# Two FFN2 pieces of the second block put ahead of those that need the last piece of w_out, and another planned length for the tails' loads

## The chip, the core and the metric

The kernel runs on one core of one Trainium2 chip. A core has a matrix engine (TensorE, PE in the profile; its weight loads are a row of their own, PEld), VectorE (DVE), ScalarE (ACT), GpSimd (POOL), and SyncE (SP), which here only issues DMAs. Matmuls write to PSUM, of which this kernel uses two banks for attention scores and six buffers, called f, for everything else. The metric is the time of one execution on the device in microseconds.

## The reference

Eight sequences of 576 positions with eight heads of 64 go through a retention layer (attention without a softmax, with a decay by distance), and its 4608 rows of 512 through a two-layer network with an ELU between.

```python
scores = scale * np.matmul(q, k.transpose(0, 1, 3, 2))
gamma = 1.0 - 2.0 ** (-5.0 - np.arange(H, dtype=np.float32))
Dmat = np.where(rel >= 0, gamma[:, None, None] ** rel[None, :, :], 0.0)
attn_out = np.matmul(scores * Dmat[None, :, :, :], v)
x = np.ascontiguousarray(attn_out.transpose(0, 2, 1, 3)).reshape(B * S, H * D)
h = x @ w_in                                                  # 512 -> 2048
g = np.where(h > 0.0, h, alpha * (np.exp(np.minimum(h, 0.0)) - 1.0))
return (g @ w_out).astype(np.float32)                         # 2048 -> 512
```

## The kernel before

**Items.** The attention is cut into items: an item is 256 positions of four heads of one sequence. Item n is loaded (q, k, v by three DMAs, or six halves from item 8 on), q and k are scaled by powers of the decay into bf16 (`qkn`, mostly on GpSimd, line 507), v is cast (`vn`, line 561), and q and k are turned into `qkT`: on TensorE for items 0 to 6 (lines 574 and 580), by a transposing DMA from SyncE for the rest (line 618). An item's step on TensorE (S5, S6, ... in the code, function `stretch`) computes scores (`sc`), the state that is carried from one part of the sequence to the next, and the output of the item before; from item 8 on two items share a step. VectorE multiplies the scores with the mask into `pt` (line 953, or 947 from item 8 on). The last 64 positions of each sequence, the tails, are two further items, 32 and 33, whose tiles lie in a buffer called `aside`. The attention output is cast into `xt`, the input of the network.

**Blocks.** The network works on blocks of 256 rows (the first six) or 512 rows, and a block T of the tails ahead of the last one. `ffn1` makes one piece of the hidden layer into an f buffer (eight matmuls of 256 columns, or four of 512), ScalarE takes the exponential (`e`, line 1161), ScalarE or VectorE a max with zero in place (lines 1169 and 1171), and VectorE combines both into `g` in bf16 (line 1176), after which the f buffer is free. `ffn2` multiplies 128 rows of g with w_out: 16 matmuls of 512 columns into one f buffer, issued as pieces of 4 (or of 2, for block 0), and ScalarE copies the sum out (line 1216) for a store by SyncE. The first eight outputs are held back in `aside` tiles and stored much later.

**Weights.** w_in and w_out come in four pieces each by DMAs that GpSimd issues and that cast to bf16 on the way. Piece n of w_out holds the rows that the matmuls 4n to 4n + 3 of each output need. FFN2 of block 0 goes through all eight of its pieces c = 0 to 7 for both of its 128-row halves in turn, so c = 6 and 7 need the last piece of w_out.

**Order.** The program does not run in the order in which it is written. Every step is an `Op` with a cost on each engine that may do it, what it depends on, and a rank. `Plan.run` plays the steps through an event list with these costs: whenever an engine is free, it takes the ready step of the lowest rank for which a buffer of each class is free (`SLOTS`, line 245; six for f), and the steps are emitted in the order in which this play began them. That fixes the order on each engine, which engine does a step that several could do, and which buffer it gets; the hardware then keeps each engine's order and waits where the data is late. All `ffn2` pieces are tied into one sequence (line 1209: each may begin only once the piece written before it has begun), and so are the loads on SyncE. A DMA has a planned length, the first number of its `dma=`: the time for which it holds its share of the DMA engines in the play. For a tail load it stands in line 467.

The two places that are edited are line 467 and the loops over `ffn2` at lines 1312 to 1324. `seq` begins with blocks 0 and 1, `TOGETHER` is 1, `rank` is the block's rank.

Of the kernel before, what the change touches and what calls it, by code (L numbers as in the profile page):

```python
# [37 lines left out]
class Plan:  # L38
# [6 lines left out]
    def add(self, *a, **kw):  # L45
        op = Op(*a, **kw)
        self.ops.append(op)
        for key in op.use:
            self.users.setdefault(key, []).append(op)
            op.turn += self.owner.get(key, [])  # L50
        for cls, key, *_ in op.take:
            self.owner[key] = [op]
            if cls not in FREE and key not in LONE:
                op.turn += self.takers.get(cls, [])
                self.takers[cls] = [op]
        return op
# [156 lines left out]
AFTER = {"ldq0_10": "tr7"}  # L213
RANKS = {"be2": 60, "be3": 60}
TOGETHER = 1
EARLY = 5
LOOSE = True
TAILS = 1
# [35 lines left out]
def kernel(  # L254
# [32 lines left out]
    def mm(*a, **kw):  # L287
        return pin(nc.tensor.matmul(*a, **kw))  # L288
# [77 lines left out]
    def T(cls, key, shape, dt):  # L366
        return (cls, key, shape, dt)

    holds, chain = [], {}
# [5 lines left out]
    for b in ORDER:  # L375
        for r in range(FT if isinstance(b, int) else 1):
            it = Item()
# [10 lines left out]
    seq = [*range(2 * NARROW), *range(2 * NARROW, 2 * B, 2)]  # L388
# [67 lines left out]
    def load_tail(it):  # L456
        n = it.n
        it.ld = {}

        def load(name, cls, key, rows, src, b, first):  # L460
            def emit(op):
                pin(nc.sync.dma_start(tiles[key][rows * ST : (rows + 1) * ST],
                                      src[b, :, FT * P :, :].rearrange("h p d -> p h d")))

            chain[0] = add(name, {"SP": 0.63}, [], emit, len(plan.ops),
                           take=[T(cls, key, [P, H, D], FP32)] if first else [], use=[] if first else [key],
                           dma=(0.93, 32), after=chain.get(0))
            return chain[0]

        for m in range(2):  # L470
            for j in range(2):
                for i, src in enumerate((q, k)):
                    it.ld[i, m, j] = load(f"ldt{i}{m}{j}{n}", "rqt", ("rqt", n, m, j), i, src, 4 * it.t + 2 * m + j, i == 0)
            for j in range(2):
                it.ld["v", m, j] = load(f"ldt2{m}{j}{n}", "rvt", ("rvt", n, m), j, v, 4 * it.t + 2 * m + j, j == 0)
# [3 lines left out]
    def load_w_in(n0, n1, after):  # L479
        c = slice(n0 * 512, n1 * 512)  # L480

        def emit(op):
            pin(nc.gpsimd.dma_start(w_in_sb[:, :, c], moe_w_in[:, c].rearrange("(j p) n -> p j n", p=P)))  # L483

        op = add(f"wi{n0}", {"POOL": 0.8}, [], emit, -1000, dma=(2.62 * (n1 - n0), 32 * (n1 - n0), PIECE), after=after)
        for n in range(n0, n1):
            w_in_ld[n] = op
# [619 lines left out]
    def early(it):  # L1107
        n = it.n
        it.sc = ("sc", n)
        sc = add(f"sc{n}", {"PE": 0.3}, it.turned, lambda op: do_scores(it), it.rank,  # L1110
                 take=[T("sc", ("sc", n), [P, 2, 512], FP32)], use=[("qkT", n)])
        mask_step(it, sc)
        keys = [("st", n, c) for c in range(2)]
        views = [(keys[c], 0, lambda c=c: tiles[keys[c]][:, :P]) for c in range(2)]
        st = add(f"st{n}", {"PE": 0.25}, [it.cq[1, 0], it.cq[1, 1], it.cv], lambda op: do_state(it, views), it.rank + 1,
                 use=[("qkn", n), ("vn", n)])
        reserve(st, keys)
        after_state(it, st, views, [(keys[0], 0), (keys[1], 0)])
# [62 lines left out]
    def rows_of(blk, it):  # L1181
        if blk == "T":
            return [(j * ST, ST, (2 * it + j) * S + FT * P) for j in range(2)]
        row = blk // 2 * S + blk % 2 * TB + it * P
        if (blk, it) in HALVED:
            return [(0, ST, row), (ST, ST, row + ST)]
        return [(0, P, row)]
# [3 lines left out]
    def ffn2(blk, it, c, per, rank, n0=0, n1=DM):  # L1191
        pkey, okey = ("p", blk, it, n0), ("ot", blk, it, n0)
        wide, cols = width[blk] > TB, n1 - n0
        gs = range(c * per, (c + 1) * per) if wide else range(c * per // 2, (c + 1) * per // 2)

        def emit(op):
            pm = tiles[pkey][:, :cols]
            for ft in range(c * per, (c + 1) * per):
                if wide:
                    g = tiles["g", blk, ft]  # L1200
                else:
                    g = tiles["g", blk, ft // 2][:, ft % 2 * TB : (ft % 2 + 1) * TB]
                mm(pm, g[:, it * P : (it + 1) * P], w_out_sb[:, ft, n0:n1], start=(ft == 0), stop=(ft == NFT - 1))

        op = add(f"F2_{blk}_{it}_{c}_{n0}", {"PE": 0.216 * per * cols / DM},
                 [gdone[blk, pp] for pp in gs] + [w_out_ld[c * per // 4]], emit, rank,
                 take=[T("f", pkey, [P, DM], FP32)] if c == 0 else [],
                 use=([pkey] if c else []) + [("g", blk, pp) for pp in gs], after=chain.get(2))
        chain[2] = op
        if (c + 1) * per == NFT:  # L1210
            late = len(deferred) < DEFER and blk != "T"
            if late:
                deferred.append(okey)

            def emit_o(op):
                pin(copy[op.eng](tiles[okey][:, :cols], tiles[pkey][:, :cols]))  # L1216

            oc = add(f"oc_{blk}_{it}_{n0}", {"ACT": 0.59 if cols == DM else 0.15 + cols / 1200,
                                             "DVE": (0.66 if cols == DM else 0.1 + cols / 960, 0.3)}, [op], emit_o, rank,
                     take=[T("late" if late else "ot", okey, [P, DM], FP32)], use=[pkey], banks=[(pkey, 0)])  # L1220

            for lo, n, i0 in rows_of(blk, it):
                def emit_s(op, lo=lo, n=n, i0=i0):
                    pin(nc.sync.dma_start(out[i0 : i0 + n, n0:n1], tiles[okey][lo : lo + n, :cols]))

                so = add(f"so_{blk}_{it}_{n0}_{lo}", {"SP": 0.46}, [oc], emit_s, -2, use=[okey],
                         dma=(0.67 * n / P * cols / DM, 8))
                if late:
                    so.at = DEFER_AT + 2.0 * len(deferred)
# [57 lines left out]
    add("warm", {"PE": 3.0}, [], emit_warm, -10 ** 6, take=[T("f", "warm", [P, 512], FP32)])  # L1287
    for it in items[:EARLY]:
        early(it)
        early_out(it)  # L1290
    for n in range(4):
        load_w_in(n, n + 1, None)
    prev, left = [], items[EARLY:]
    while prev or left:
# [13 lines left out]
    for i, blk in enumerate(seq):  # L1308
        if i > 1:
            for p in range(NFT if width[blk] > TB else NP):  # L1310
                ffn1(blk, p, base[blk] + 2 * p)
        rank = base[blk] + width[blk] // 16 + 1
        if i < TOGETHER:
            if i == 0:
                for c in range(8):
                    for b in seq[:TOGETHER]:
                        for it in range(2):
                            ffn2(b, it, c, 2, rank + 2 * c)
        else:
            for it in range(width[blk] // P):  # L1320
                cuts = LAST if (i, it) == (len(seq) - 1, width[blk] // P - 1) else (0, DM)
                for n0, n1 in zip(cuts, cuts[1:]):
                    for c in range(4):
                        ffn2(blk, it, c, 4, rank + 8 * it + 2 * c, n0, n1)

    for op in plan.ops:
# [74 lines left out]
```

## Time and profile before

| | us |
|---|---|
| median of 3 runs | 299.19 (299.08 to 302.05) |
| the profiled execution | 299.32 |
| its span, first to last instruction | 297.6 |
| TensorE busy | 291.2 |
| ScalarE busy | 197.9 |
| VectorE busy | 181.1 |
| GpSimd busy | 133.7 |
| moved by DMA | 50.12 MB |

The granted TensorE clock is 1.0 throughout. A row of a timeline gives the start, the time from the first start to the last end, engine, line, operation, what is written and read, shapes, and how many instructions of the kind followed one another; in brackets stands the idle time of the engine before it and what ended it. The end of a matmul is modelled and overlaps the start of the next, so distances are better taken from start to start. A row of the table of waits gives who waited for whom, the sum in us, how often, and the longest. A row of the table by windows gives the stretch and its length, then busy time and count of PE, PEld, DVE, ACT and POOL, the granted clock, the DMA share and GB/s. "To landing" is the time from the issue of a DMA to the arrival of its data.

### The profile page before, as it was taken

How to read it: one execution, taken by the hardware profiler on the slowest of the kernel's cores; microseconds unless marked ns; L12 is line 12 of the kernel's file. 1: busy time of each engine (PE TensorE's matmuls, PEld its weight loads, DVE VectorE, ACT ScalarE, POOL GpSimd, SP SyncE). 2: the span in 40 equal slices, each digit the busy share in tenths (PEclk: the TensorE clock that was granted, in tenths of full speed). 3: DMA queues.
4: the chain of work that ended last, by engine and by line, in shares of the span. 5: the costliest groups of instructions: out<-in, count | busy, mean ns of one | idle time of the engine just before them, and what ended most of it. 6: DMA issues, size and time to landing. Idle time of an engine off the chain costs nothing.

```text
span 297.6 us, 8805 instructions
## 1 busy us (share of the span) xinstructions
PE 291.2 (98%) x3518; PEld 162.3 (55%) x3518; DVE 181.1 (61%) x323; ACT 197.9 (66%) x393; POOL 133.7 (45%) x253
## 2 busy tenths in 40 slices
PE   7999989999999999999999999999999999999996
PEld 3578646765776664545545454545454544444445
DVE  5999924947856948697855946466550169643300
ACT  2679624858767758778786868686772289777512
POOL 5961279956755856567442827372533000000000
PEclk9999999999999999999999999999999999999999
DMA  7999999989999999999999998976577310011132
GB/s 205 273 205 214 216 274 226 194 181 170 182 178 195 196 231 209 184 223 213 247 255 260 214 191 203 210 176 150 125 161 176 73 35 4 0 35 36 37 106 71
DMA packets 142010, 50.12 MB, mean 168 GB/s; under 512 B 120721, under 2 KB 137489, under 8 KB 141969
## 3 DMA queue, kind: packets, MB, share of 16 engines
q1 hardware_dynamic: 137744, 45.37, 71.3%
q0 software_dynamic: 4224, 4.19, 8.4%
q8 instruction: 27, 0.44, 0.6%
q14 instruction: 15, 0.11, 0.1%
HBM read 36.70 MB, written 9.44 MB: 155 GB/s over the span
## 4 chain that ended last, share of the span: by engine, by line
PE 85%; DMA 7%; DVE 3%; POOL 2%; issue 1%; ACT 0%; ACTq 0%; DVEq 0%
PE f L288 83%; DMA w_out_sb<-in_moe_w_out_dram 7%; PE sc L288 2%; DVE pt L953 1%; POOL w_out_sb L491 1%; PE f L574 1%; POOL w_in_sb L483 1%; DVE g L1176 0%; DVE qkn L507 0%; DVE qkT L580 0%; DVE s_mid L850 0%; POOL s_mid L836 0%; POOL s_end L836 0%; DVE f L1171 0%; ACT e L1161 0%
## 5 line engine op out<-in xcount | busy, mean ns | idle before, releaser
L288 PE MATMUL f<-w_out_sb,g 128*128 128x512 bf16 (+2 forms) x608 | 141.2, 368 | 1.0 <-DMA w_out_sb<-in_moe_w_out_dram 1.0
L288 PE MATMUL f<-xt,w_in_sb 128*128 128x256 bf16 (+1 forms) x768 | 138.4, 326 | 0.4 <-DVE g L1176 0.4
L1176 DVE SCALAR_TENSOR_TENSOR g<-e,f 128x512 bf16<-128x512 f32 x144 | 95.4, 683 | 65.2 <-ACT f L1169 51.5
L1161 ACT ACTIVATE e<-f 128x512 f32<-128x512 f32 x144 | 84.6, 597 | 35.2 <-PE f L288 27.0
L288 PEld LDWEIGHTS <-w_in_sb 128*128 128x128 bf16 x768 | 74.5, 98 | 54.2 <-DVE g L1176 0.9
L288 PEld LDWEIGHTS <-g 128*128 128x128 bf16 x608 | 56.6, 98 | 58.8 <-issue 1.3
L1169 ACT ACTIVATE f<-f 128x512 f32<-128x512 f32 x113 | 66.6, 592 | 0.0
L507 POOL TENSOR_TENSOR qkn<-rqk,far_k 128x256 bf16<-128x256 f32 x48 | 29.0, 611 | 11.4 <-DMA rqk<-in_k_dram 10.6
L507 POOL TENSOR_TENSOR qkn<-rqk,far_q 128x256 bf16<-128x256 f32 x48 | 28.7, 611 | 6.0 <-DMA rqk<-in_q_dram 5.1
L1216 ACT COPY ot<-f 128x512 f32<-128x512 f32 (+2 forms) x30 | 16.9, 562 | 20.5 <-PE f L288 20.4
L561 POOL CAST vn<-rv 128x512 bf16<-128x512 f32 x28 | 17.0, 609 | 20.2 <-DMA rv<-in_v_dram 20.0
L893 POOL CAST y<-mid 64x256 bf16<-64x256 f32 x33 | 12.8, 398 | 25.4 <-DVE mid L878 8.9
L988 ACT CAST xt<-f 128x512 bf16<-128x512 f32 x24 | 12.9, 589 | 15.1 <-PE f L288 15.1
L1171 DVE TENSOR_SCALAR f<-f 128x512 f32<-128x512 f32 x31 | 21.3, 694 | 2.5 <-ACT e L1161 2.4
L947 DVE TENSOR_TENSOR pt<-sc,mask_t 128x1024 bf16<-128x1024 f32 x12 | 14.6, 1219 | 3.2 <-PE sc L288 3.2
L893 ACT CAST y<-mid 64x256 bf16<-64x256 f32 x33 | 12.8, 402 | 1.8 <-DVE mid L878 0.9
L634 POOL TENSOR_TENSOR aside<-aside,gq 128x256 bf16<-128x256 f32 x16 | 9.4, 611 | 10.0 <-DMA aside<-in_k_dram 9.8
L507 POOL TENSOR_TENSOR qkn<-rqk,gq 128x256 bf16<-128x256 f32 x12 | 7.4, 630 | 11.9 <-DMA rqk<-in_q_dram 11.9
L878 DVE TENSOR_TENSOR mid<-f,mid 128x256 f32<-128x256 f32 x24 | 10.2, 424 | 2.5
L288 PE MATMUL f<-pt,vn 64*64 64x64 bf16 (+1 forms) x512 | 11.6, 202 | 0.0
L953 DVE TENSOR_TENSOR pt<-sc,mask 128x1024 bf16<-128x1024 f32 x8 | 9.8, 1222 | 2.0 <-PE sc L288 1.9
L288 PE MATMUL f<-zero 128*128 128x512 bf16 (+3 forms) x30 | 9.2, 416 | 1.3 <-DVE zero L293 1.3
(91 smaller groups left out, 165.6 us busy)
## 6 DMA issues: line engine op xcount, KB each, us to landing
rqk<-in_q_dram SPq DMA_DIRECT2D x48, 128.0 KB, 3.2
rqk<-in_k_dram SPq DMA_DIRECT2D x48, 128.0 KB, 3.5
rv<-in_v_dram SPq DMA_DIRECT2D x48, 128.0 KB, 3.5
out_dram<-ot SPq DMA_DIRECT2D x18, 256.0 KB, 3.1
out_dram<-ot SPq DMA_DIRECT2D x19, 128.0 KB, 2.3
rqk<-in_q_dram SPq DMA_DIRECT2D x8, 256.0 KB, 6.0
rqk<-in_k_dram SPq DMA_DIRECT2D x8, 256.0 KB, 5.5
rv<-in_v_dram SPq DMA_DIRECT2D x8, 256.0 KB, 5.4
```

Source lines behind the costliest of these rows:

```text
L288: return pin(nc.tensor.matmul(*a, **kw))
L507: pin(alu[op.eng].tensor_tensor(dst, tiles[raw][:, :, e], g, ALU.mult))
L561: pin(copy[op.eng](tiles["vn", n], tiles["rv", n]))
L893: pin(copy[op.eng](dst, tiles[key][j * D : (j + 1) * D]))
L947: pin(nc.vector.tensor_tensor(tiles[it.pt].rearrange("p i h n -> p (i h n)")[:, : 2 * w * C].rearrange("p (i x n) -> p i x n", i=2, n=C), ...
L953: pin(nc.vector.tensor_tensor(tiles["pt", n].rearrange("p i h n -> p (i h) n"), tiles[it.sc].rearrange("p i (h n) -> p (i h) n", h=2), mas ...
L988: pin(copy[op.eng](by_block(it.xt)[:, 2 * it.T + c], tiles[xkey, c].rearrange("p (h n) -> p h n", n=P)))
L1161: pin(nc.scalar.activation(tiles[ekey], tiles[hkey], AF.Exp))
L1169: pin(nc.scalar.activation(ph, ph, AF.Relu))
L1171: pin(nc.vector.tensor_scalar_max(ph, ph, 0.0))
L1176: pin(nc.vector.scalar_tensor_tensor(tiles[gkey], tiles[ekey], -1.0, tiles[hkey], ALU.add, ALU.min))
L1216: pin(copy[op.eng](tiles[okey][:, :cols], tiles[pkey][:, :cols]))
```

## The change

Two pieces of the first 128 rows of block 1, four matmuls each with the first two pieces of w_out, are written ahead of pieces c = 6 and 7 of block 0, with a rank that lies just ahead of theirs, and left out of their old place. Apart from that, the planned length of a tail load goes from 0.93 to 0.8; it is a number of the play alone, and the DMA moves the same bytes.

```diff
@@ -213,6 +213,7 @@
 TOGETHER = 1
+HEAD = 2
 EARLY = 5
@@ -464,7 +465,7 @@
             chain[0] = add(name, {"SP": 0.63}, [], emit, len(plan.ops),
                            take=[T(cls, key, [P, H, D], FP32)] if first else [], use=[] if first else [key],
-                           dma=(0.93, 32), after=chain.get(0))
+                           dma=(0.8, 32), after=chain.get(0))
             return chain[0]
@@ -1313,6 +1314,8 @@
         if i < TOGETHER:
             if i == 0:
                 for c in range(8):
+                    for k in range(HEAD if c == 6 else 0):
+                        ffn2(seq[1], 0, k, 4, rank + 11)
                     for b in seq[:TOGETHER]:
                         for it in range(2):
                             ffn2(b, it, c, 2, rank + 2 * c)
@@ -1320,7 +1323,7 @@
             for it in range(width[blk] // P):
                 cuts = LAST if (i, it) == (len(seq) - 1, width[blk] // P - 1) else (0, DM)
                 for n0, n1 in zip(cuts, cuts[1:]):
-                    for c in range(4):
+                    for c in range(HEAD if (i, it) == (1, 0) else 0, 4):
                         ffn2(blk, it, c, 4, rank + 8 * it + 2 * c, n0, n1)
```

Since the play is one, the order changes beyond the two pieces. TensorE has the same instructions in both kernels; up to the moved pieces its order is the same, and behind them FFN1 pieces, FFN2 pieces and items' steps change places at some forty points to the end. Of the steps that more than one engine may do, one max pass goes from VectorE to ScalarE and two casts of attention states go from GpSimd to ScalarE. On SyncE, loads, transposes and stores swap places at some twenty points from item 9 on.

## The prediction

> **What bounds the kernel now.** I read the page's busy shares and its chain first, then who TensorE waited for, then TensorE's own timeline around each wait.
>
> ```profile
> span 297.6 us, 8805 instructions
> PE 291.2 (98%) x3518; PEld 162.3 (55%) x3518; DVE 181.1 (61%) x323; ACT 197.9 (66%) x393; POOL 133.7 (45%) x253
> ...
> PE 85%; DMA 7%; DVE 3%; POOL 2%; issue 1%; ACT 0%; ACTq 0%; DVEq 0%
> ```
>
> ```profile
> PE f L288 <- DMA w_out_sb<-in_moe_w_out_dram: 1.0, 1, 1.0
> PE f L288 <- DVE g L1176: 0.4, 1, 0.4
> ```
>
> ```profile
> 222.41 12.25 PE L288 MATMUL f<-w_out_sb,g 128*128 128x512 bf16 x56
> 234.49 0.40 PE L288 MATMUL f<-aside,s_end 128*128 128x64 bf16 x8
> ```
>
> TensorE is busy for 98% of the span, and the chain that ended last runs through it for 85%. After the start-up its table of waits holds two entries that cost anything: one for the last piece of w_out, one for VectorE's g. The last two rows, from TensorE's timeline, say what saturated means: 56 matmuls of 512 columns in 234.49 - 222.41 = 12.08 us, so one starts every 0.216 us; a piece of FFN2 (four matmuls) is 0.863 us. Work moved about on TensorE costs nothing and gains nothing; only a filled wait counts, and only if no new one opens. With the start-up alike, the gain is bounded by the two waits.
>
> The Trainium skill ("Perfetto Trace Analysis", Identifying the Most-Contended Engine) says that matmul busy time is a poor measure and that the share of LDWEIGHTS should be taken; by its 55% TensorE would have much room, and a filled wait could be swallowed elsewhere. The 0.216 us pitch speaks against that here, so I carry a filled wait through to the end.
>
> **The first wait.**
>
> ```profile
> 38.97 0.61 PE L288 MATMUL f<-w_out_sb,g 128*128 128x512 bf16 x2
> 40.55 1.89 PE L288 MATMUL f<-w_out_sb,g 128*128 128x512 bf16 x8 [0.97 <-DMA w_out_sb<-in_moe_w_out_dram]
> 42.27 0.39 PE L574 MATMUL f<-ident,qkn 128*128 128x128 bf16 x4
> 42.49 1.03 PE L288 MATMUL f<-w_out_sb,g 128*128 128x512 bf16 x4
> ...
> 44.53 0.42 PE L288 MATMUL sc<-qkT 64*64 64x128 bf16 x16
> ...
> 45.01 0.40 PE L574 MATMUL f<-ident,qkn 128*128 128x128 bf16 x4
> ...
> 47.20 0.27 PE L288 MATMUL f<-qkT,s_mid 128*128 128x128 bf16 x2
> ```
>
> ```profile
> 18.81 21.69 DMA w_out_sb<-in_moe_w_out_dram
> 40.50 0.04 issue
> ```
>
> The chain shows the DMA of w_out's last piece landing at 40.50. TensorE's last two matmuls before it start at 38.97 and 0.216 later, so the next could start at 39.40; it starts at 40.55. The idle column says 0.97 because a matmul's end is modelled; counted from start to start 1.15 us are lost. The change puts 2 x 4 matmuls of block 1 there: 8 x 0.216 = 1.73 us, to 41.13, past the landing. They need pieces 0 and 1 of w_out (their matmuls ran before in this stretch for block 0), g of block 1, made before FFN2 began, and a PSUM buffer.
>
> ```profile
> 37.22 0.29 DVE L819 COPY mid<-f 128x128 f32<-128x128 f32 x1 [0.41 <-PE f L288]
> ...
> 39.58 1.18 POOL L507 TENSOR_TENSOR qkn<-rqk,gq 128x256 bf16<-128x256 f32 x2 [0.81 <-DMA rqk<-in_q_dram]
> 41.18 1.18 POOL L507 TENSOR_TENSOR qkn<-rqk,gk 128x256 bf16<-128x256 f32 x2 [0.41 <-DMA rqk<-in_k_dram]
> ...
> 42.88 1.18 POOL L507 TENSOR_TENSOR qkn<-rqk,gq 128x256 bf16<-128x256 f32 x2
> ```
>
> The buffer it is given was last read by VectorE's mid copy, done at 37.51: free. So the first wait goes whole. What is late next are the transposes, which the pieces now overtake: by the changed order TensorE does q of item 5, two half pieces of block 0 (4 matmuls), k of item 5, four more matmuls, the scores and states of item 5, then q of item 6. A transpose takes 42.49 - 42.27 = 0.22 us, item 5's step 45.01 - 44.53 = 0.48. Step by step: q at 41.13 (GpSimd done 40.76: no wait), 41.35 + 0.86 = 42.21; k's product is done at 41.18 + 1.18 = 42.36, so about 0.2 us of wait; with it 42.41 + 0.22 + 0.86 + 0.48 = 43.97; q of item 6 is done at 42.88 + 1.18 = 44.06, about 0.1 us more. Then 0.22 + 1.73 + 0.22 + 0.86 brings TensorE to item 6's step at 47.1, where it stood at 47.20 before, with one FFN2 piece more behind it: a lead of 0.86 + 0.1, about **0.9 us**. These two small waits hang on loads that arrive with a scatter of their own: without the two DMA waits shown on GpSimd (0.81 and 0.41) they would be nothing, with both as long again they would grow by up to 1.2. I keep 0.3, the rows' own, and both ends for the range. No other step of the stretch (the casts of xt, the copy of the first output) came near to TensorE's need in this reckoning.
>
> **The second wait.** The shift changes the order some 25 us later, by the scheduler's doing: before, three FFN1 pieces of block 3 precede the step of items 8 and 9, then the fourth, the last FFN2 piece of block 2's first half, and the wait; after, that FFN2 piece comes ahead, two FFN1 pieces precede the step and three follow it.
>
> ```profile
> 49.84 6.28 PE L288 MATMUL f<-xt,w_in_sb 128*128 128x256 bf16 x56
> 55.95 1.03 PE L288 MATMUL f<-w_out_sb,g 128*128 128x512 bf16 x4
> ...
> 62.84 2.78 PE L288 MATMUL f<-xt,w_in_sb 128*128 128x256 bf16 x24
> 65.55 0.45 PE L288 MATMUL sc<-qkT 64*64 64x64 bf16 x32
> ...
> 66.19 1.05 PE L288 MATMUL f<-xt,w_in_sb 128*128 128x256 bf16 x8
> 67.08 1.03 PE L288 MATMUL f<-w_out_sb,g 128*128 128x512 bf16 x4
> 68.49 1.05 PE L288 MATMUL f<-xt,w_in_sb 128*128 128x256 bf16 x8 [0.39 <-DVE g L1176]
> ```
>
> ```profile
> 65.69 0.69 DVE L1171 TENSOR_SCALAR f<-f 128x512 f32<-128x512 f32 x1
> 66.30 1.22 DVE L947 TENSOR_TENSOR pt<-sc,mask_t 128x1024 bf16<-128x1024 f32 x1
> ...
> 67.76 0.68 DVE L1176 SCALAR_TENSOR_TENSOR g<-e,f 128x512 bf16<-128x512 f32 x1
> ```
>
> ```profile
> 64.98 1.28 ACT L1161 ACTIVATE e<-f 128x512 f32<-128x512 f32 x2
> ...
> 66.67 0.38 ACT L876 COPY mid<-f 128x256 f32<-128x256 f32 x1
> ```
>
> TensorE is through at 67.08 + 0.86 = 67.94 and goes on at 68.49: 0.55 us lost, until the g of block 3's second piece frees a buffer. Ahead of that g VectorE runs a max pass (65.69 to 66.30) and the mask of items 8 and 9. In the changed order the max pass of this piece is on ScalarE and the mask follows directly, so g starts 0.61 earlier and TensorE's release falls at 68.49 - 0.61 = 67.88. ScalarE can have that max done: half of the two e passes from 64.98 to 65.62, the mid copy 0.38, a pass as long as an e, 0.64: 66.64, ahead of g at 67.15. TensorE itself arrives at 62.84 + 5 FFN1 pieces at (55.95 - 49.84) / 7 = 0.873 + 0.64 for the step (66.19 - 65.55) = 67.85. So 0.03 us of the 0.55 are left: gain **0.5 us**. Bounds: nothing, if VectorE keeps its old pace, and 0.55.
>
> **The shorter planned length** (0.93 to 0.8 for a tail load) moves no byte. It changes places in the queue of SyncE: stores of outputs and transposes of the tails swap with loads, and the tails' scaling on GpSimd gets ahead of the casts it stood behind. The second tail's step now precedes three FFN2 pieces that it followed. TensorE's work is the same, so at nothing if the loads are there; the cover is counted below. Two casts go from GpSimd to ScalarE (66% busy): nothing.
>
> **Sum**, on the profiled execution's 299.32 us (span 297.6, 1.7 around it): 0.9 + 0.5 = 1.4, so 297.9; the median of the three runs is 299.19, 0.13 below it, so **297.8 us**.
>
> **The rivals.**
>
> ```profile
> 109.63 0.49 PE L288 MATMUL sc<-qkT 64*64 64x64 bf16 x32
> ```
>
> ```profile
> L618 SPq DMA_TRANSPOSE qkT<-qkn x1: 1289/1289/1289, 104.0 to 104.0; - x1
> ...
> DMA to landing us min/median/max: 4.3/4.3/4.3
> ```
>
> ```profile
> 100.00:110.00 10.00, 10.00 (x143) 6.34 (x144) 5.88 (x10) 6.43 (x13) 6.39 (x13) 1.00 1.14 198
> ```
>
> *The lead runs into the transposes.* The qkT of item 17 lands at 104.0 + 4.3 = 108.3, its scores start at 109.63: 1.3 us of room against a lead of 1.4, while the DMA share of that stretch stands at 1.14. If the transposes keep their time TensorE waits about 0.1 there; if they slip by 0.5 to 1 us, as much of the lead is given back: 298.3 to 298.9. For it: the loads set the transposes' time. Against it: SyncE's queue is reordered too, and items' buffers come free earlier with TensorE. The Trainium skill ("DMA: Bandwidth & Descriptors", Issuing engines are not separate DMA queues) says that all issuers share the same 16 DMA engines, by which a transpose would not come sooner because TensorE is; the trace's share agrees that they are full.
>
> *Only the first wait goes*, because the new order parks another step in front of that g: 299.19 - 0.9 = 298.3.
>
> ```profile
> 235.05 0.45 PE L288 MATMUL sc<-aside 64*64 64x64 bf16 x32
> ```
>
> ```profile
> L644 SPq DMA_TRANSPOSE aside<-aside x1: 1250/1250/1250, 228.7 to 228.7; - x1
> ...
> DMA to landing us min/median/max: 2.5/2.5/2.5
> ```
>
> *The tail is taken too early* (slower). The second tail's scores start at 235.05; their last transpose lands at 228.7 + 2.5 = 231.2, 3.9 us of room. Three pieces less in front and the lead of 1.4 take 2.6 + 1.4 = 4.0 of it. TensorE goes in order, so a late transpose stops everything behind it. If they land when they did, TensorE, there at 231.05, waits 0.15; from a landing 1.3 us later on the change is a loss, and one 3 us later gives 299.2 - 1.4 + 3.15 = 300.9. Against it: the tails' scaling is no longer behind the casts, so the transposes should be issued earlier, not later.
>
> *The change doesn't do what it says*: the pieces wait for a buffer or for g. The mid row speaks against it; 299.2.
>
> **Chances.** Forecast 0.66 (its own range 297.3 to 298.3: no small waits on one side; the second gain halved or small waits of 0.8 on the other); transposes 0.15; only the first wait 0.08; tail 0.07; no effect 0.04. The range reaches to the transposes' case and a little past no change: 297.3 to 299.3. About 1% is what a measurement of this kernel can tell from no change; the two waits together are 1.7 us, 0.6%, so faster by over 1% gets 0.01, slower by over 1% (302.2, a tail some 4.3 us late) 0.03, within 0.96.
>
> **What would show it.** Right: no wait of TensorE on w_out; FFN2 matmuls without a gap through 39.4; k of item 5 at about 42.4; g's wait near 68 at 0.1 or less; from 70 on no start-to-start gap, the last copy 1.4 us earlier. Wrong: a new wait of TensorE on qkT near 72 to 110 or on the tail's aside near 231, or any row in TensorE's table of waits over 0.3 us after 45.

## The result, and the profile after

| | before | after |
|---|---|---|
| median of 19 runs each | 299.60 us (298.69 to 302.05) | 298.26 us (297.33 to 303.42) |
| ratio of the times, 95% interval | | 0.9954 (0.9935 to 0.9974) |
| the profiled execution | 299.32 us | 297.93 us |
| its span | 297.6 us | 296.2 us |

The changed kernel is 0.5% faster: 1.34 us between the medians, 1.4 us between the two profiled executions. A ratio of 1 lies outside the interval, so there is a gain, though it is smaller than the 1% that the prediction took as visible. The ratio goes by the fast runs, without the one of 303.42 us, in which the granted clock was 0.989.

The page of the changed kernel, its busy shares and its chain:

```profile
PE 290.5 (98%) x3518; PEld 162.2 (55%) x3518; DVE 178.4 (60%) x322; ACT 198.6 (67%) x396; POOL 133.7 (45%) x251
...
PE 94%; DMA 2%; POOL 1%; DVE 1%; SPq 0%; issue 0%; ACT 0%; ACTq 0%; POOLq 0%
```

The busy shares hardly moved; a table of shares would not have shown that anything happened. The chain did: DMA went from 7% to 2% of it and TensorE from 85% to 94%. TensorE's whole table of waits (who waited for whom, sum, times, longest):

```profile
PE f L289 <- DVE zero L294: 1.3, 1, 1.3
PE f L575 <- POOL qkn L508: 0.6, 3, 0.3
PE sc L289 <- DVE qkT L581: 0.3, 1, 0.3
PE f L289 <- DVE pt L954: 0.2, 1, 0.2
```

Neither w_out nor g stands in it any more. What is left belongs to the start-up: behind 18 us no two neighbouring matmuls of TensorE start further apart than their columns explain. (The lines of the changed kernel are one higher than those of the kernel before.)

TensorE's timeline where it waited for w_out:

```profile
39.27 2.33 PE L289 MATMUL f<-w_out_sb,g 128*128 128x512 bf16 x10
41.44 0.39 PE L575 MATMUL f<-ident,qkn 128*128 128x128 bf16 x4
...
42.53 0.39 PE L575 MATMUL f<-ident,qkn 128*128 128x128 bf16 x4
...
47.23 0.27 PE L289 MATMUL f<-qkT,s_mid 128*128 128x128 bf16 x2
```

Ten FFN2 matmuls now stand in one row, at 41.44 - 39.27 = 2.17 us for ten starts: the old pitch of 0.216 with no hole. And where it waited for g, TensorE first, then VectorE:

```profile
65.36 2.79 PE L289 MATMUL f<-xt,w_in_sb 128*128 128x256 bf16 x24
67.99 1.03 PE L289 MATMUL f<-w_out_sb,g 128*128 128x512 bf16 x4
68.85 1.04 PE L289 MATMUL f<-xt,w_in_sb 128*128 128x256 bf16 x8
```

```profile
65.73 1.22 DVE L948 TENSOR_TENSOR pt<-sc,mask_t 128x1024 bf16<-128x1024 f32 x1
66.87 0.41 DVE L879 TENSOR_TENSOR mid<-f,mid 128x256 f32<-128x256 f32 x1
67.20 0.68 DVE L1177 SCALAR_TENSOR_TENSOR g<-e,f 128x512 bf16<-128x512 f32 x1
```

g is done at 67.20 + 0.68 = 67.88, and the piece of four behind the FFN1 pieces starts at 67.99 and ends 0.86 later: four times the pitch, no wait. The max pass that stood on VectorE ahead of the mask is gone from this stretch.

So the two waits were filled, as foreseen, and the two profiled executions add up: 1.15 + 0.55 us of waits gone, less 0.30 us by which TensorE came later out of the start-up (39.27 against 38.97), are 1.40, as the spans have it (297.6 - 296.2). The open questions were these. Does each part of the change do what the prediction ascribed to it? Is the planned length really worth nothing? And does the gain survive to the end only because TensorE is saturated, or does something else in the new order protect it?

### The profile page after: what moved, and what is told of

The parts are those of the page before. It is cut to its first block, busy times and chain, and to the rows that moved or that the text cites. A ratio compares the mean times of both kernels' runs of the same rounds, so it can differ in the third digit from the quotient of the medians.

```text
span 296.2 us, 8815 instructions
## 1 busy us (share of the span) xinstructions
PE 290.5 (98%) x3518; PEld 162.2 (55%) x3518; DVE 178.4 (60%) x322; ACT 198.6 (67%) x396; POOL 133.7 (45%) x251
## 4 chain that ended last, share of the span: by engine, by line
PE 94%; DMA 2%; POOL 1%; DVE 1%; SPq 0%; issue 0%; ACT 0%; ACTq 0%; POOLq 0%
PE f L289 91%; PE sc L289 2%; DMA rqk<-in_q_dram 2%; PE f L575 1%; POOL qkn L508 1%; SPq L435 0%; DVE pt L954 0%; POOL w_in_sb L484 0%; DVE qkn L508 0%; POOL s_mid L837 0%; POOL s_end L837 0%; DVE qkT L581 0%; DVE s_mid L851 0%; DVE end L829 0%; ACT ot L1217 0%
## 5 line engine op out<-in xcount | busy, mean ns | idle before, releaser
L1172 DVE TENSOR_SCALAR f<-f 128x512 f32<-128x512 f32 x30 | 20.5, 694 | 2.8 <-ACT e L1162 2.6
```

Of the source, the lines that this page charges most:

```text
L1172: pin(nc.vector.tensor_scalar_max(ph, ph, 0.0))
```

## Experiments: the two parts alone, and each wait alone

**The two pieces without the new planned length.**

```diff
-                           dma=(0.8, 32), after=chain.get(0))
+                           dma=(0.93, 32), after=chain.get(0))
```

> The two pieces moved, the tails' loads planned at 0.93 as before. Both theories expect the first two waits gone as in the changed kernel: no wait of TensorE on w_out at 39.4 and none on g near 68, TensorE 1.4 us ahead by 72 us. Theory A (the planned length matters through the order it gives at the tail): in this order no FFN2 piece is left between the output of the second tail item and the first FFN1 piece of block T, so TensorE waits there for the casts of xt, about 0.9 us (before: output's last matmul ends near 238.37, first FFN1 piece at 239.28, with one FFN2 piece of 0.86 between); the gain is 1.4 - 0.9 = 0.5 us, ratio 0.998. Rival B (the length is only a number of the plan and costs nothing): gain 1.4 us, ratio 0.9955, no wait at block T.

Measured: 298.90 us, ratio 0.9983 (0.9969 to 0.9996). Both old waits are gone, and a new one stands at the end of the second tail. TensorE's timeline there:

```profile
238.26 0.45 PE L289 MATMUL f<-pt,aside 64*64 64x64 bf16 x32
239.54 1.68 PE L289 MATMUL f<-xt,w_in_sb 128*128 128x512 bf16 x7 [0.84 <-DVE xt L1005]
```

The tail's output is followed at once by FFN1 of block T, whose input is that very output: TensorE waits until VectorE has cast it. The 32 matmuls of the output take 0.37 us in the changed kernel (below), so TensorE could go on at 238.63 and does at 239.54: 0.9 us. In the changed kernel, the same place reads:

```profile
234.03 0.44 PE L289 MATMUL f<-pt,aside 64*64 64x64 bf16 x32
234.40 1.90 PE L289 MATMUL f<-w_out_sb,g 128*128 128x512 bf16 x8
236.14 4.05 PE L289 MATMUL f<-xt,w_in_sb 128*128 128x512 bf16 x18
```

Two FFN2 pieces cover the cast. So the pieces alone use up the cover that hid it, and the other planned length is what brings the cover back. A second loss of 0.72 us in this trace was a wait for a transposing DMA at items 8 and 9. The traced execution, at 299.6 us, is slower than the median of this run, which lies 0.6 us below that of the kernel before (299.52).

**The new planned length without the pieces.**

```diff
-HEAD = 2
+HEAD = 0
```

> Only the planned length 0.8, no piece moved. Theory A: both waits of the kernel before stay (start to start 1.15 us lost at 39.4 and 0.55 near 68), the tail had no gap to lose: ratio 1.000, within 0.2 us. Rival B: part of the changed kernel's gain comes from the tail, ratio 0.997 to 0.999.

Measured: 299.71 us, ratio 1.0011 (0.9994 to 1.0029). Nothing, as expected: both old waits stand (0.96 and 0.55 us start to start), and TensorE's table of waits has nothing on the tail. It lost 0.7 us to a transpose at items 14 and 15, which the changed kernel did not.

**The first wait alone, in the order of the kernel before.** Block 0's last four hidden tiles are multiplied with the third piece of w_out, which is there long before the last one.

```diff
+                wt = ft - 4 if blk == 0 and ft >= 12 else ft
-                mm(pm, g[:, it * P : (it + 1) * P], w_out_sb[:, ft, n0:n1], start=(ft == 0), stop=(ft == NFT - 1))
+                mm(pm, g[:, it * P : (it + 1) * P], w_out_sb[:, wt, n0:n1], start=(ft == 0), stop=(ft == NFT - 1))
```

> The order of the kernel before on every engine, but FFN2 of block 0 multiplies its last four hidden tiles with the third piece of w_out in place of the fourth, so that nothing at 39.4 us waits for the last piece (the output of block 0 is not the reference's). Theory A (TensorE is saturated, a filled wait is carried to the end): no wait on w_out; TensorE reaches item 5's transposes 1.15 us earlier and is held there by GpSimd for some tenths; the wait near 68 stays at 0.55; gain 0.8 to 1.1 us, ratio 0.9965 to 0.997. Rival B (the lead is swallowed by a later chain, transposes or VectorE): a new wait after 45 us, gain under 0.4, ratio 0.999 or more.

Measured: 298.76 us, ratio 0.9983 (0.9967 to 1.0000). The wait on w_out is gone and the one on g stays, but only about 0.5 us arrives. TensorE's table of waits has a new entry:

```profile
PE f L288 <- DVE g L1176: 0.4, 1, 0.4
PE sc L288 <- DMA qkT<-qkn: 0.3, 1, 0.3
```

Of the 1.15 us, 0.92 were left at item 6's step (46.28 against 47.20): the other 0.23 went to waits for q and k of items 5 and 6, the small waits of the prediction. A further 0.43 us went to the transposes (start to start at the scores of items 18 and 19), and the 0.49 that remain are the difference of the spans (297.1 against 297.6). The last is the rival of the prediction, in the old order. I had not expected it at this size here: the result is between the two theories.

## Experiments: what made the second wait go

**The max pass alone moved to ScalarE.**

```diff
+        if op.name == "md_3_1":
+            op.eng = "ACT"
         op.emit(op)
```

> The order of the kernel before, with the max pass of block 3's second piece done by ScalarE, at its place in the order, in place of VectorE; nothing else. Theory A: the mask of items 8 and 9 starts 0.6 us earlier on VectorE, so g of that piece too, and the wait of TensorE near 68 falls from 0.55 to 0.1 or less; the wait on w_out stays at 1.15; gain 0.5 us, ratio 0.998 to 0.9985. Rival B (g is held by something else, or ScalarE's extra pass delays the next piece): the wait stays or moves to the next FFN1 piece, ratio 1.000.

Measured: 299.72 us, ratio 1.0006 (0.9991 to 1.0021). The expectation was missed: the wait on g is longer, not shorter. TensorE's, VectorE's and ScalarE's timelines of this run:

```profile
67.33 1.03 PE L288 MATMUL f<-w_out_sb,g 128*128 128x512 bf16 x4
68.88 1.05 PE L288 MATMUL f<-xt,w_in_sb 128*128 128x256 bf16 x8 [0.53 <-DVE g L1176]
```

```profile
66.31 1.23 DVE L947 TENSOR_TENSOR pt<-sc,mask_t 128x1024 bf16<-128x1024 f32 x1 [0.28 <-PE sc L288]
67.81 0.42 DVE L878 TENSOR_TENSOR mid<-f,mid 128x256 f32<-128x256 f32 x1 [0.27 <-ACT mid L876]
68.15 0.68 DVE L1176 SCALAR_TENSOR_TENSOR g<-e,f 128x512 bf16<-128x512 f32 x1
```

```profile
66.40 1.08 ACT L1169 ACTIVATE f<-f 128x512 f32<-128x512 f32 x2
67.39 0.39 ACT L876 COPY mid<-f 128x256 f32<-128x256 f32 x1
```

The 0.6 us that VectorE saved it spent waiting: 0.28 for the scores, which TensorE still gives late, and 0.27 for ScalarE's mid copy, which now stands behind the max pass. An engine relieved of work does not run ahead if what it does next comes from an engine that was not moved.

**The scores earlier**, as in the changed order (the step of items 8 and 9 ahead of the third FFN1 piece of block 3, and ScalarE's mid copy ahead of an e pass), first without, then with the max pass on ScalarE. `ahead` puts the named steps directly ahead of another in the order in which they are emitted.

```diff
+    ahead(("S8b0", "S8b1", "S8"), "F1_3_2")
+    ahead(("mid0_8",), "ex_3_2")
```

```diff
+    ahead(("S8b0", "S8b1", "S8"), "F1_3_2")
+    named["md_3_1"].eng = "ACT"
+    ahead(("mid0_8", "md_3_1"), "ex_3_2")
```

> The order of the kernel before, with the step of items 8 and 9 one FFN1 piece earlier on TensorE and ScalarE's copy of its first state ahead of the next exponential; the max pass of block 3's second piece stays on VectorE. Theory A (the wait near 68 needs both moves of the changed order: the max pass away from VectorE and the scores earlier): VectorE still does g, max, mask, mid, g in a row from 65.1, so g of the second piece starts near 67.8 and the wait stays at 0.5 to 0.55. Theory B (the early scores alone did it): wait 0.1 or less.

> As the run before, and the max pass on ScalarE too. Theory A: mask right behind g of the first piece, g of the second piece 0.6 us earlier, wait near 68 at 0.1 or less, w_out's wait unchanged at about 1.15; gain 0.5 us, ratio 0.998 to 0.9985. Theory B (g is held by the copy of the state or by ScalarE): the wait stays at 0.5.

Measured, scores alone: 300.67 us in a single execution; the wait on g stands at 0.55 us as before, so the scores alone do nothing for it (the run also lost 0.90 us to a transpose). With both: 299.24 us, ratio 0.9995 (0.9971 to 1.0018). The wait on g is gone, but one stands a piece later. TensorE and ScalarE:

```profile
68.58 1.03 PE L288 MATMUL f<-w_out_sb,g 128*128 128x512 bf16 x4
69.76 1.03 PE L288 MATMUL f<-xt,w_in_sb 128*128 128x256 bf16 x8 [0.16 <-ACT aside L1216]
```

```profile
69.13 0.59 ACT L1216 COPY aside<-f 128x512 f32<-128x512 f32 x1
```

TensorE could go on at 68.58 + 0.86 = 69.44 and does at 69.76: 0.33 us for the buffer that ScalarE copies out until 69.72, the output of block 2's first half. In the changed kernel this half's last FFN2 piece comes before the step of items 8 and 9 and ScalarE's copy stands at 63.08. So the two moves together took 0.22 of the 0.55 us, where neither took any alone, and the changed order, which also has that FFN2 piece earlier, took the rest. That this third move is what takes the rest is read from ScalarE's rows; no run made it alone.

## Experiments: who keeps the gain

**The waits on w_out and on g filled, in an order otherwise that of before** (the last edit together with that of the w_out piece).

> As the run before, and block 0 uses the third piece of w_out in place of the fourth for its last four hidden tiles (its output is not the reference's). Theory A (the changed kernel's whole gain is these two waits): both gone, order otherwise that of the kernel before; gain 1.3 to 1.5 us less what TensorE waits for q and k of items 5 and 6 (0.1 to 0.4): ratio 0.9955 to 0.9965. Theory B (half of the gain comes from the rest of the new order): ratio 0.998.

Measured: 299.02 us, ratio 0.9983 (0.9964 to 1.0003). No wait on w_out or g, and yet less than half of the gain. The wait for ScalarE's copy of the run before is still there (0.33 us start to start at 69.19), so 1.15 + 0.22 = 1.37 us could have been gained. From TensorE's table of waits, and its timeline at the scores of items 14 and 15:

```profile
PE sc L288 <- DMA qkT<-qkn: 1.7, 3, 1.0
...
PE f L288 <- ACT aside L1217: 0.2, 1, 0.2
```

```profile
94.98 0.31 PE L288 MATMUL sc<-qkT 64*64 64x64 bf16 x14
96.33 0.32 PE L288 MATMUL sc<-qkT 64*64 64x64 bf16 x16 [1.04 <-DMA qkT<-qkn]
```

TensorE came 1.2 us earlier than in the kernel before (where the scores stand at 96.14 in one row of 30) and stood still until 96.33. The transpose did not come earlier with it. The answer on its line gives the durations of the issue in ns and its start, and below that the time to landing; first this run, then the kernel before:

```profile
L618 SPq DMA_TRANSPOSE qkT<-qkn x1: 2501/2501/2501, 90.7 to 90.7; - x1
...
DMA to landing us min/median/max: 5.6/5.6/5.6
```

```profile
L618 SPq DMA_TRANSPOSE qkT<-qkn x1: 1378/1378/1378, 90.5 to 90.5; - x1
...
DMA to landing us min/median/max: 5.0/5.0/5.0
```

Before, it landed at 90.5 + 5.0 = 95.5, 0.6 us ahead of the scores; here at 96.3. A lead of more than that room is lost. With two shorter ones (0.44 and 0.57 us at items 18 and 20) the transposes cost 2.2 us in this trace, and 297.6 - 1.37 + 2.2 = 298.4 is its span. The traced execution, 300.12 us, is one of the two slowest of twelve; the median lost less.

**The same with the transposes' lateness taken away.** Items 14 to 21 compute with the `qkT` of the pair before, which landed long ago; TensorE does the same instructions.

```diff
-        tt = tiles["qkT", n]
+        tt = tiles["qkT", n - 2 if 14 <= n < 22 else n]
```

> As the kernel with both waits taken away in the order before (its profile lost 1.2, 0.44 and 0.57 us at the scores of items 14, 18 and 20 to their transposes), but the scores of items 14 to 21 read the qkT of the pair before, which has landed long ago (so they are not the reference's). Theory A (the lead was eaten by transposes that land when they land): these waits go, nothing takes their place, and the gain is what the changed kernel has: 1.2 to 1.5 us, ratio 0.995 to 0.9965. Rival B (the old order loses the lead elsewhere as well, to v, to VectorE or to ScalarE): new waits of the same size, ratio 0.998 or more.

Measured: 298.46 us, ratio 0.9961 (0.9935 to 0.9987), span 296.4: a gain of the changed kernel's size is back, and TensorE's table of waits has no transposing DMA. TensorE's scores at the same place:

```profile
94.99 0.45 PE L288 MATMUL sc<-qkT 64*64 64x64 bf16 x29
```

So in the old order the transposes take the difference: the sum above shows it for the traced execution, and the medians of the two runs agree with it. The medians alone do not prove it, since the two intervals overlap, and in this second trace item 15's own transpose landed at 91.7 + 3.4 = 95.1, early enough that hardly anything would have been lost there. Why do the transposes not take it in the changed kernel? The stretches up to the first matmul of that step, from the table by windows of the kernel before and of the changed one (us, PE busy and count, PEld, DVE, ACT, POOL, clock, DMA share, GB/s):

```profile
0.00:95.74 95.74, 92.15 (x1278) 61.92 (x1278) 68.72 (x146) 61.52 (x129) 61.52 (x117) 1.00 1.07 209
```

```profile
0.00:95.99 95.99, 93.16 (x1290) 62.87 (x1290) 68.74 (x144) 63.06 (x134) 61.82 (x118) 1.00 1.00 210
```

TensorE has done 12 matmuls more by then: one FFN2 piece of four and one FFN1 piece of eight, 0.86 + 0.87 = 1.73 us of work. It stands 0.25 us later than before, not 1.4 earlier. The re-planned order puts that step two network pieces later, so the lead is held as work done ahead and not as earliness against a DMA. Its transpose, issued at 91.3, landed 3.5 us later, at 94.8, and the scores came at 96.39.

The order gives this step 1.6 us of room, but the landing helped too: at 94.8 the transpose was there even for a TensorE that came at 94.98, as in the run with both waits filled. And not every step is held back: at items 16 and 17 the changed kernel comes earlier than the kernel before, with its scores at 108.15 against 109.63, and there the transpose landed at 103.4 + 4.2 = 107.6, 0.5 us ahead of them. No run tells apart how much of the escape is the order and how much the landing in those executions. Two runs whose order is close to the changed kernel's did lose time to transposes: 0.72 us above at items 8 and 9, and 0.4 us in the next one.

**One piece instead of two.**

```diff
-HEAD = 2
+HEAD = 1
```

> The changed kernel with one piece moved ahead in place of two (0.86 us of work against 1.15 us of wait); planned length 0.8. Theory A (behind the filled wait TensorE is held by GpSimd's q and k of items 5 and 6 anyway): about 0.3 us of wait on w_out stay, but TensorE meets q and k of items 5 and 6 later, so it stands at item 6's step at the same time; ratio as for two pieces, 0.9955 within 0.001. Theory B (the second piece is worth its 0.3 us): ratio 0.9965.

Measured: 298.26 us, ratio 0.9966 (0.9947 to 0.9985). Its interval overlaps that of two pieces, so the times do not tell the theories on the second piece apart. The trace does, for one execution:

```profile
39.40 2.55 PE L289 MATMUL f<-w_out_sb,g 128*128 128x512 bf16 x10
41.79 0.39 PE L575 MATMUL f<-ident,qkn 128*128 128x128 bf16 x4
```

Ten starts take 41.79 - 39.40 = 2.39 us here, and 2.17 with two pieces: inside the row TensorE stood 0.22 us, until w_out's last piece landed at 40.89, a DMA that this run's chain goes through (7%). Item 6's step starts at 47.57, 8.17 us behind the row's start, against 47.23 - 39.27 = 7.96 in the changed kernel with the same work between. So the 0.22 us was not made up by meeting q and k later, as theory A has it; the second piece was worth what the first one left, as theory B has it. A further 0.4 us was lost for a transpose at items 16 and 17.

**Repeats**, to see the scatter of single executions: the kernel before once, the changed kernel twice.

> The kernel before once more. Theory A: the two waits again, about 1.1 and 0.55 us start to start; and at the scores of items 14, where the first profile had 0.6 us of room, a wait on the transpose of up to 0.9 or none, as the landing scatters by more than a microsecond from run to run. Rival: never a wait there.

> The changed kernel once more. Theory A: no wait on w_out, none over 0.1 near 68; waits on transposes seldom, at the scores of items 8, 10, 16 or 20, which the new order puts earlier, and none at items 14 and 18, which it puts one piece later; sum of TensorE's waits after 20 us under 0.8. Rival: transposes cost as much as before.

> The changed kernel a third time, to see the scatter; theory A: no wait on w_out, none over 0.1 near 68, waits on transposes seldom and under 0.8 us in sum. Rival: as much as before.

The kernel before, in this execution 301.31 us with a span of 299.6, has both known waits and one more:

```profile
PE sc L288 <- DMA qkT<-qkn: 1.2, 1, 1.2
PE f L288 <- DMA w_out_sb<-in_moe_w_out_dram: 1.0, 1, 1.0
...
PE f L288 <- DVE g L1176: 0.4, 1, 0.4
```

The first one lies at the scores of items 22 and 23 (1.4 us start to start), where the trace of before had none: the kernel before runs close to its transposes even without any lead. The changed kernel gave 297.50 us (span 295.8, again with no wait on a DMA or on g, and none on the transposes) and 301.69 us, of which the last section tells.

## Why the prediction was right, and where its steps were not

The forecast was 297.8 us and a gain of 1.4; the median is 298.26, the profiled execution 297.93 against the 297.9 of the sum, and the gain 1.34 to 1.4. Step by step:

- **What bounds the kernel** held. TensorE's pitch, not the share of its weight loads, was the thing to read: PEld is at 55% before and after, and the filled waits came through to the end. The Trainium skill ("Perfetto Trace Analysis", Identifying the Most-Contended Engine) names that share together with MFU, the floating-point work done as a share of the peak; the prediction weighed the share of the weight loads alone. Taken alone it would have seen room, and the trace disagrees with that reading.
- **The first wait** went whole, by the row of ten. Item 6's step was forecast at 47.1 with one FFN2 piece more behind it; it came at 47.23, where the stretches up to it, of the kernel before and of the changed one, count 548 and 552 matmuls:

```profile
0.00:47.19 47.19, 43.99 (x548) 28.09 (x549) 35.80 (x90) 26.36 (x59) 26.52 (x53) 1.00 1.09 232
```

```profile
0.00:47.22 47.22, 44.39 (x552) 28.33 (x553) 36.21 (x90) 26.84 (x60) 26.96 (x54) 1.00 1.10 233
```

- **The two small waits** of 0.3 us were mis-sized: in the changed kernel they did not open. In the profiled execution TensorE came into this stretch 0.30 us later than before (39.27 against 38.97), by its start-up, and k of item 5 was ready at 42.45, just ahead of its transposition at 42.53. In the second trace of the changed kernel the start-up was as early as before (38.99), and k was ready sooner, at 40.55 + 1.19 = 41.74; again no wait, item 6's step at 46.95, and the span 295.8, that is 1.8 us below the span before. So with start-ups alike the gain in these traces is nearer to 1.15 + 0.55 than to 1.4, and the sum met the profiled time by luck: the late start-up was as long as the waits that I had put in. That the waits can open is shown by the run with the third piece of w_out, where TensorE came to q at 41.14 and lost 0.23 us.

```profile
40.55 1.19 POOL L508 TENSOR_TENSOR qkn<-rqk,gk 128x256 bf16<-128x256 f32 x2 [0.44 <-DMA rqk<-in_k_dram]
```

- **The second wait** was right in size (0.5 forecast, 0.55 gained) and in place (the release by g forecast at 67.88 and TensorE's arrival at 67.85; g's end at 67.88 and TensorE's next piece at 67.99 measured). Its cause was told too shortly. "The max pass is on ScalarE, so g starts 0.61 earlier" is not enough: the max pass alone gained nothing, the scores alone gained nothing, and both together left 0.33 us of it, on a buffer that ScalarE's output copy held. The changed order makes all three moves; the working reckoned with the max pass and with the pieces that TensorE does ahead of the wait, and did not ask when the scores are there for the mask nor when the copy frees its buffer.
- **The planned length at nothing** is right against the kernel before (ratio 1.0011) and wrong as a part of this change. Without it the pieces lost 0.9 us at block T in the trace. What the prediction said of it, that the second tail's step now precedes FFN2 pieces that it followed, was weighed only as a risk; it is also the cover of the cast that follows.
- **The rival of the transposes**, at 0.15, was a real mechanism and not a remote one: a single wait of this kind cost 0.4 to 1.2 us in the traces of six of the experiments, and 1.4 in the repeat of the kernel before. I counted the room at items 16 and 17 (1.3 us), while items 14 and 15 had only 0.6. The three traces of the changed kernel show no such wait. Its order holds the step of items 14 and 15 two pieces back, which the working did not see; but there and at items 16 and 17, where the room was 0.5 us, the transposes also landed early enough, and that part is luck.
- **Only the first wait**, **too early a tail** and **no effect** did not come. The second tail's scores stood at 231.09 where 231.05 was forecast, and TensorE's table of waits has nothing on the tail.

What stays open: whether the 0.2 us of the second piece shows in the median, how much of the escape from the transposes is the order, and what single execution times above 301 us consist of in general; only two of them were traced.

## What to carry to other kernels

On a saturated engine a filled wait is worth its start-to-start length, but only if the engine then does not arrive early at something that a DMA sets: list every late-landing transfer behind the wait with its room, and go by the smallest room, not by one. Where the order turns a lead into work done ahead of a DMA-bound step, as at items 14 and 15 here, the step's room is not used up. When a change is re-planned by a scheduler, compare the orders step by step, and test the parts alone and together: here the planned length was worth nothing alone, and 0.9 us beside the pieces, in the trace.

## What the runs showed of the hardware that was not expected

In the slowest traced execution of the changed kernel (span 300.0) one load of v came late in the start-up, and TensorE stood still for it. Its timeline, and the table by windows behind it (us, PE busy and count, PEld, DVE, ACT, POOL, clock, DMA share, GB/s):

```profile
17.70 0.23 PE L289 MATMUL f<-zero 128*128 128x128 bf16 x1
20.11 0.43 PE L289 MATMUL f<-vn,qkn 64*64 64x64 bf16 x16 [2.18 <-ACT vn L562]
20.47 3.23 PE L289 MATMUL f<-xt,w_in_sb 128*128 128x256 bf16 x16
```

```profile
18.00:19.00 1.00, 0.00 (x0) 0.09 (x1) 1.00 (x1) 0.00 (x0) 1.00 (x2) 1.00 1.23 206
19.00:20.00 1.00, 0.00 (x0) 0.00 (x0) 0.05 (x1) 0.56 (x2) 0.91 (x3) 0.88 1.26 210
21.00:22.00 1.00, 1.00 (x7) 0.69 (x6) 0.92 (x3) 0.00 (x0) 0.00 (x0) 0.50 1.22 200
```

The idle time cost 2.35 us, and then the granted clock was 0.50 from about 20 to 23 (and 1.00 again from 24 on): 16 matmuls of 256 columns took 3.06 us from start to start (the next row begins at 23.53) where they otherwise take 16 x 0.109 = 1.75. The wait was paid more than once and a half: 2.35 + 1.3 for these 16 alone, of the 4.2 us by which this span exceeds the other repeat's. The Trainium skill ("TensorE: Matmul & The Clock Gate", What's actually happening) gives half rate after at least one idle window of about 3.4 us and full rate after as long a busy time. The half rate agrees with this trace; the idle time does not, since 2.35 us between two starts were enough here. It is one execution, and TensorE was busy for only 0.66 to 0.93 of each microsecond from 14 to 18, with waits of its own; no run separates the one idle stretch from that. The waits of 1.15 and 0.55 us that the change filled did not set the clock down: it was 1.0 throughout.

The second surprise is the scatter of one transpose. The same transfer (that of item 15), issued at 90.5 to 91.3, took 5.0 us to land in the kernel before, 5.6 with both waits filled, and 3.5 in the changed kernel. The spread, 2.1 us, is larger than the whole gain of this change.
